# Split buffers of g in two pools, one key scaling a step sooner, attention of block 0 in 27 half steps, and one block's output stores on another queue

## The chip, the cores and the metric

The kernel runs on one core of a Trainium2 chip. The metric is the device time of one execution in microseconds (us). The five engines that matter are TensorE (PE in the profile; its weight loads are PEld), VectorE (DVE), ScalarE (ACT), GpSimd (POOL) and SyncE (SP, which here only issues transfers). Each engine works through its own list of instructions in order, and an instruction that has to wait holds up everything behind it on that engine. ACT and SP both issue transfers (ACTq and SPq in the rows).

## The reference, cut to what matters

```python
# attention with decay: 4 sequences of 576 tokens, 8 heads of 64
scores = scale * np.matmul(q, k.transpose(0, 1, 3, 2))
Dmat = np.where(rel >= 0, gamma[:, None, None] ** rel[None, :, :], 0.0)
ret = scores * Dmat[None, :, :, :]
attn_out = np.matmul(ret, v)
x = attn_out.transpose(0, 2, 1, 3).reshape(B * S, H * D)      # 2304 x 512
# layer one, 512 -> 2048 -> 512
h = x @ w_in;  g = h * (1.0 / (1.0 + np.exp(-h)));  x = g @ w_out
# layer two, the same sizes with its own weights
h = x @ w_in;  g = np.maximum(h, 0.0) ** 2;         out = g @ w_out
```

## The kernel before, in words

The 2304 tokens are cut into 18 *units* of 128 tokens. Attention is computed unit by unit with a running state S (`scores_step`: products of keys and queries into P, mask, new state; `values_step`: products with the values into Q, which become a unit's columns of x).

Products that must keep fp32 accuracy are done in three float32r passes: each operand is split into a high part (`xh`, `gh`, `wi`; a cast on ACT) and a low part (`xl`, `gl`; a subtraction on DVE or POOL), and TensorE adds high*high, high*low and low*high. Where the program has a helper for this it is `split` (L690 to L692): a cast on ACT at once, and a subtraction that is put on the list `later`/`low` and emitted with the next work.

**Layer one, first part.** Three *blocks* of tokens, `BLOCKS = [512, 384, 384]` (units 0 to 3, 4 to 6, 7 to 9). For each block and each of 16 slices f of the hidden width, `gemm1` makes `ph` (12 matmuls, L83), ACT and DVE gate and split it, and two slices later `gemm2` adds it to `acc` (12 matmuls, L83). Each slice has two *half steps*: `gemm1` stands ahead of the first, `gemm2` in the second. During block 0 the weights are converted from 64-bit numbers, one tile each half step: stage a (two ACT operations, L115 and L116), b (three DVE operations, L121 to L123), c (ACT cast, L135), d (DVE subtraction, L139). The attention of the next block's units runs beside the current block: `run_att` does as many attention steps as the fraction of half steps that has passed. Block 0 carries the six steps of units 4 to 6, whose x is the input of block 1.

`prep_k(u)` scales the keys of unit u: one POOL operation (L351) for one half of the heads and four ACT operations (L354) for the other. The second group of products in `scores` (L369) needs them; the first group (L364) doesn't. For unit 4 it stands in the loop over slices.

In the last slice of a block `gemm2` copies the four `acc` tiles to y (L665, DVE and ACT in turn) and ACT issues their stores (L666).

**Layer one, second part** (from about 302 us): the remaining 1024 tokens with seven block products in place of eight (L761), after sums and splits of x (`xsa`).

**Layer two** works in the same seven-product form. Its first phase (L901) makes g, which goes out to DRAM from the tiles `g` of pool "gq" (L940, `gD<-g`, on SP). Its second phase (L990) loads g back (`gr<-gD`, L952), sums and splits it (`sum_g`, `split_g`) and multiplies it with the split sums of the weights (`w2s`). There are 9 groups P of token rows with 7 products i each. Which split is emitted beside which product is decided by the small planner at the end: every entry has a step at which it is due and a cost, and each product adds 3.6 to the room. The tiles that `split_g` writes come from a pool "hl" of six buffers that is opened when x's pool "xp" and the pools of the first phase are closed; so these buffers lie where x and the g tiles lay, and the first instruction that writes one waits until the old content is no longer read.

Of the kernel before, what the change touches and what calls it, by code (L numbers as in the profile page):

```python
# [8 lines left out]
F32R = mybir.dt.float32r  # L9
# [15 lines left out]
KD, KF = DM // 128, DFF // 128  # L25
BLOCKS = [512, 384, 384]
# [17 lines left out]
def kernel(  # L44
# [16 lines left out]
    nc = tc.nc  # L61
# [18 lines left out]
    def mm3(o, pairs, first=True, last=True):  # L80
        n = len(pairs)
        for i, (a, b) in enumerate(pairs):
            mm(o, a, b, start=first and i == 0, stop=last and i == n - 1)  # L83
# [61 lines left out]
    def flush():  # L145
        now = later[:]
        later.clear()
        for emit in now:
            emit()
# [6 lines left out]
    def keep_w(n):  # L156
        layer, f, part = w_at(n)
        if part == 0:
            t = first.pop(n) if n in first else conv[n][0]
            nc.sync.dma_start(out=w1f[f // 2, :, f % 2], in_=t.bitcast(F32))  # L160
# [10 lines left out]
    def conv_to(layer, n):  # L171

        for i in range(conv_n[layer], min(n, 2 * KF + 2)):
            conv_n[layer] += 1
            for lag, stage in ((2, conv_c), (0, conv_a), (1, conv_b), (2, conv_d)):
                if 0 <= i - lag < 2 * KF:
                    stage(layer * 2 * KF + i - lag)
                    if stage is conv_b and n_loaded[0] < i - lag + layer * 2 * KF + RAW + 1:
                        load_next()
                    if stage is conv_b:  # L180
                        keep_w(i - lag)
# [53 lines left out]
    def pre_step():  # L235

        step = pre_n[0]
        pre_n[0] += 1
        for n, at in enumerate(pre_at):
            k = step - at  # L240
            if k == 0:
                pre_load(n)
            elif k == 2:
                conv_a(("p", n, 0))
            elif k == 3:
                conv_b(("p", n, 0))
                conv_a(("p", n, 1))
            elif k == 4:
                conv_b(("p", n, 1))
            elif k in (5, 6):  # L250
                pre_sums(n, k - 5)
            elif k == 7:
                pre_store(n)
# [71 lines left out]
    def load(u, queue=nc.sync):  # L325
        if u < NU:
            new_raw(u)
            for g in range(NG):
                queue.dma_start(out=raw[u][g], in_=att[NG * u + g])
# [15 lines left out]
    def prep_k(u):  # L345

        for g in range(NG):
            kn = raw[u][g][:, 256:512].rearrange("p (h d) -> p h d", h=4)
            w = (Tkn_u if u < n_start else Tkn)[:, 4 * g : 4 * g + 4]
            if g == 0 and u < u_end[1]:  # L350
                nc.gpsimd.tensor_mul(kn, kn, w.unsqueeze(2).to_broadcast([128, 4, D]))  # L351
            else:
                for h in range(4):
                    nc.scalar.activation(kn[:, h], kn[:, h], ACTF.Copy, scale=w[:, h : h + 1])  # L354
# [261 lines left out]
    x2 = dp.tile([128, KD, NT], F32, name="x2")  # L616
    tok0 = [sum(BLOCKS[:j]) for j in range(len(BLOCKS))]
    ph_t = {}

    def gemm1(layer, j, f, c0=0, c1=None):  # L620

        n = BLOCKS[j]
        c1 = c1 or n
        if c0 == 0:
            ph_t[layer, j, f] = ps_g.tile([128, 512], F32, tag="g", name="ph")[:, 0:n]
        ph = ph_t[layer, j, f][:, c0:c1]
        wh, wl = wt[0, f][:, 0], wt[0, f][:, 1]
        xh, xl = x_t[j]
        for k in range(KD):
            w0 = slice(k * 128, k * 128 + 128)  # L630
            mm3(
                ph,
                [(wh[:, w0], xh[:, k, c0:c1]), (wh[:, w0], xl[:, k, c0:c1]), (wl[:, w0], xh[:, k, c0:c1])],
                first=k == 0 and c0 == 0,
                last=k == KD - 1 and c1 == n,
            )
        if c1 == n:
            later.append(lambda: gate(layer, j, f, ph_t.pop((layer, j, f))))
# [11 lines left out]
    def gemm2(layer, j, f):  # L650
        n = BLOCKS[j]
        gh, gl = g_t.pop((layer, j, f))
        wh, wl = wt[1, f][:, 0], wt[1, f][:, 1]
        if f == 0:
            acc[layer, j] = [ps_o.tile([128, 512], F32, tag="o", name="acc") for _ in range(KD)]
        for t in range(KD):
            o = acc[layer, j][t][:, 0:n]
            w0 = slice(t * 128, t * 128 + 128)
            pairs = [(wh[:, w0], gh), (wh[:, w0], gl), (wl[:, w0], gh)]
            mm3(o, pairs, first=f == 0, last=f == KF - 1)  # L660
            if f == KF - 1:
                if t % 2 == 0:
                    ys = rp.tile([128, 2, 512], F32, tag="wr", name="y")
                y = ys[:, t % 2, 0:n]
                (nc.scalar.copy if t % 2 else nc.vector.tensor_copy)(y, o)  # L665
                nc.scalar.dma_start(out=x2[:, t, tok0[j] : tok0[j] + n], in_=y)  # L666

# [6 lines left out]
    pools = {}  # L676
# [13 lines left out]
    def split(dst, src, engine=nc.vector):  # L690
        nc.scalar.copy(dst[0], src)  # L691
        low.append(lambda: engine.tensor_sub(dst[1], src, dst[0]))  # L692
# [43 lines left out]
    def ts_step(p, k):  # L736
        if k == 0:
            ts_load(p)
        elif k in (2, 3):
            ts_sum(p, k - 2)  # L740
        elif k == 5:
            ts_split(p)
# [199 lines left out]
    def wait(n, emit):  # L942
        later.append(emit if n == 0 else lambda: wait(n - 1, emit))

    g_raw = {}
    g_s = {}
    g_l = {}
# [21 lines left out]
    def split_g(P, i, pool, engine=nc.vector):  # L969
        src = g_s[P][i]  # L970
        if pool == "w":
            parts = [wp.tile([128, 2, 512], F32R, tag="w", name="gl") for _ in range(2)]
            for e, t in enumerate(parts):
                split((t[:, 0], t[:, 1]), src[:, 512 * e : 512 * e + 512], engine)
        else:
            t = pools[pool].tile([128, 2, 1024], F32R, tag="h", name="gl")
            split((t[:, 0], t[:, 1]), src)
            parts = [t[:, :, 0:512], t[:, :, 512:1024]]
        g_l[P, i] = parts
# [76 lines left out]
    nb = len(BLOCKS)  # L1056
# [30 lines left out]
    def run_att(upto):  # L1087
        while pos[0] < min(upto, len(att_steps)):
            u, step = att_steps[pos[0]]
            step(u)  # L1090
            pos[0] += 1

    def att_end(j):
        return 2 * (u_end[j] - n_start)
# [55 lines left out]
    for i in range(len(seq) + LAG):  # L1150
        if i < len(seq):
            layer, j, f = seq[i]
            if i == 0:
                for c in ((0, AHEAD), (AHEAD, BLOCKS[0])):
                    for ff in range(2):
                        gemm1(layer, j, ff, *c)
            elif i > 1:
                gemm1(layer, j, f)
            if i == 0:
                for n in range(W1_FIRST):  # L1160
                    keep_w(n)
            if i == 1:
                load(n_start + 1)
            if i == 2:
                prep_k(n_start)
        for half in range(2):
            step = 2 * (i - (nb - 1) * KF) + half
            if step >= 0:
                flush()
            if i < len(seq):  # L1170
                if j == 0:
                    conv_to(0, 2 * f + half + 1 + W1_AHEAD)
                if j == 1 or step == 0:
                    pre_step()
                if j == 1 and half == 0:
                    nc.sync.dma_start(out=woD[f], in_=wt[1, f].bitcast(F32))
                if j == nb - 1:
                    for p in range(5):
                        ts_step(p, step - 4 * p - 3)
            if step >= 0:  # L1180
                strassen_x(step)
            if step < 0:
                flush()
            if half and i >= LAG:
                gemm2(*seq[i - LAG])
            if i < len(seq):
                a0, a1 = att_end(j), att_end(j + 1)
                run_att(a0 + (a1 - a0) * (2 * f + half + 1) // (2 * KF - 3 if j < nb - 1 else 22))
    flush()
    flush()  # L1190
    gp_ctx.close()
# [32 lines left out]
    for n in range(2 * KF):  # L1224
        h, f = divmod(n, KF)
# [19 lines left out]
    def new_pool(stack, name, bufs):  # L1245
        pools[name] = stack.enter_context(tc.tile_pool(name=name, bufs=bufs, reuse_waits="tile"))
# [28 lines left out]
    l1_ctx.close()  # L1275
    xp_ctx.close()
    lp_ctx.close()
    for name, bufs in (("hl", 6), ("rq", 6), ("tq", 1)):
        new_pool(ctx, name, bufs)


# [16 lines left out]
    for P in range(1, NPP):  # L1298
        n = 7 * P
# [6 lines left out]
    for P in range(1, NPP):  # L1306
        for q, at in ((2, -10), (3, -10), (0, -9), (1, -8)):
            pool, tag = ("w", "w") if q == 2 and P > 1 else ("rq", "r")
# [87 lines left out]
```

## Time and profile before

| | |
|---|---|
| time, median of 3 runs | 844.78 us (843.49 to 845.17) |
| the profiled execution, its own time | 838.52 us |
| span of the profile | 836.7 us |
| matmuls and weight loads | 6410 each |
| 128x512 fp32 products of one slice in block 0 | 12 for `ph`, 12 for `acc` |

The times of the rows below are us from the start of the span of this one execution. In a row of the timeline the first number is the start, the second the time from the start of the first to the end of the last instruction of the row, `x12` how many were merged, and the brackets at the end hold how long the engine sat idle before it and what released it. Instructions that only issue a transfer are not counted as busy time. PEclk is the clock that TensorE was granted, 1.00 for 2.4 GHz and 0.50 for 1.2 GHz.

### The profile page before, as it was taken

What the parts mean: (1) busy time and instruction counts of PE and PEld (TensorE: products, weight loads), DVE (VectorE), ACT (ScalarE), POOL (GpSimd) and SP (SyncE); (2) the same over time, 40 slices, a digit from 0 to 9 for tenths busy, and PEclk for the clock granted to TensorE, in tenths of its full rate; (3) what the DMA queues carried; (4) which work ended last, traced back from release to release, by engine and by line L of the source; (5) the groups of instructions that cost most, each with busy time, mean ns of one, the idle gap of its engine ahead of it and who ended that gap; (6) DMA issues with size and microseconds to landing.
All of it is one profiled execution on the core that took longest, in us unless ns stands there. A gap on an engine that the chain in (4) does not pass through costs nothing.

```text
span 836.7 us, 16174 instructions
## 1 busy us (share of the span) xinstructions
PE 812.1 (97%) x6410; PEld 751.6 (90%) x6410; DVE 548.0 (65%) x809; ACT 451.4 (54%) x862; POOL 186.0 (22%) x204
## 2 busy tenths in 40 slices
PE   6899999999999999999999999999999899999998
PEld 5788878999988988888888999999999789999998
DVE  5899994545434556666778577546477688777772
ACT  6777774454455455464555575646577434433430
POOL 3202012324544213213431222303254000000000
PEclk9989999999999999999999999999999999999999
DMA  9777775888534022698795465352676833444300
GB/s 353 255 229 240 253 225 201 310 308 298 190 128 153 1 78 87 222 313 309 225 344 184 154 225 165 122 171 92 202 275 213 310 139 126 140 134 136 122 27 26
DMA packets 71980, 160.70 MB, mean 192 GB/s; under 512 B 6112, under 2 KB 37344, under 8 KB 71904
## 3 DMA queue, kind: packets, MB, share of 16 engines
q1 hardware_dynamic: 66432, 149.44, 52.4%
q10 hardware_dynamic: 5472, 10.23, 3.3%
q8 instruction: 50, 0.82, 0.4%
q14 instruction: 26, 0.21, 0.1%
HBM read 104.07 MB, written 55.57 MB: 191 GB/s over the span
## 4 chain that ended last, share of the span: by engine, by line
PE 77%; DVE 3%; ACT 2%; issue 1%; DMA 1%; POOL 0%; ACTq 0%; DVEq 0%
PE acc L83 18%; PE pa L901 12%; PE pa L990 11%; PE pb L901 9%; PE pb L990 8%; PE ph L83 8%; PE pa L761 5%; PE pb L761 4%; PE Q L415 1%; DMA gD<-g 1%; PE P L364 1%; DVE xsa L692 1%; PE P L369 1%; ACT raw L354 1%; DVE gl L692 0%
## 5 line engine op out<-in xcount | busy, mean ns | idle before, releaser
L83 PE MATMUL ph<-xh,wi 128*128 128x384 f32 (+2 forms) x400 | 115.3, 351 | 1.3 <-ACT xh L457 1.3
L83 PE MATMUL acc<-gh,wo 128*128 128x384 f32 (+1 forms) x384 | 115.5, 362 | 0.0
L990 PE MATMUL pa<-w2s,gl 128*128 128x256 f32 x864 | 110.3, 285 | 4.0 <-ACT y L1005 3.0
L990 PEld LDWEIGHTS pa<-w2s,gl 128*128 128x128 f32 x864 | 107.1, 194 | 4.8 <-ACT y L1005 3.2
L901 PE MATMUL pa<-xa,w1s 128*128 128x384 f32 x576 | 105.9, 335 | 0.0
L901 PEld LDWEIGHTS pa<-xa,w1s 128*128 128x128 f32 x576 | 100.4, 188 | 0.1
L691 ACT CAST gl<-gr 128x1024 fp32r<-128x1024 f32 (+1 forms) x57 | 55.9, 1002 | 60.8 <-DVE gr L965 21.4
L83 PE MATMUL acc<-gsl,wo 128*128 128x512 f32 x384 | 87.7, 390 | 0.0
L83 PEld LDWEIGHTS acc<-gsl,wo 128*128 128x128 f32 x384 | 72.0, 188 | 15.5
L990 PE MATMUL pb<-w2s,gl 128*128 128x256 f32 x648 | 82.5, 283 | 1.6 <-ACT gl L691 0.8
L990 PEld LDWEIGHTS pb<-w2s,gl 128*128 128x128 f32 x648 | 79.7, 192 | 2.0 <-ACT gl L691 1.0
L901 PE MATMUL pb<-xa,w1s 128*128 128x384 f32 x432 | 80.9, 335 | 0.0
L83 PEld LDWEIGHTS ph<-xh,wi 128*128 128x128 f32 x400 | 73.2, 188 | 7.1 <-ACT xh L457 1.7
L83 PEld LDWEIGHTS acc<-gh,wo 128*128 128x128 f32 x384 | 71.8, 191 | 6.4
L901 PEld LDWEIGHTS pb<-xa,w1s 128*128 128x128 f32 x432 | 75.5, 188 | 0.1
L692 DVE TENSOR_TENSOR gl<-gr,gl 128x1024 fp32r<-128x1024 f32 (+1 forms) x55 | 64.7, 1181 | 13.5 <-ACT gl L691 13.5
L83 PE MATMUL ph<-xl,wi 128*128 128x384 f32 (+2 forms) x200 | 69.6, 348 | 0.3 <-DVE xl L461 0.3
L83 PE MATMUL acc<-gl,wo 128*128 128x384 f32 (+1 forms) x192 | 68.7, 358 | 0.0
L115 ACT ACTIVATE t<-wr 128x512 f32<-128x512 f32 x64 | 43.0, 672 | 26.6 <-DMA wr<-w 26.4
L648 DVE TENSOR_TENSOR gl<-sg,gh 128x384 fp32r<-128x384 f32 (+1 forms) x48 | 29.9, 623 | 40.5 <-ACT gh L647 40.5
L645 ACT ACTIVATE sg<-ph 128x384 f32<-128x384 f32 (+1 forms) x48 | 25.1, 524 | 53.1 <-PE ph L83 52.6
L122 DVE CUSTOM_DVE_ANT_0 t<-wr,t 128x1024 uint16<-128x1024 uint16 x64 | 47.6, 744 | 8.0 <-ACT sg L645 0.5
(140 smaller groups left out, 1334.5 us busy)
## 6 DMA issues: line engine op xcount, KB each, us to landing
wr<-w SPq DMA_DIRECT2D x64, 512.0 KB, 4.5
gD<-g SPq DMA_DIRECT2D x48, 384.0 KB, 2.8
gr<-gD SPq DMA_DIRECT2D x36, 512.0 KB, 4.7
raw<-att SPq DMA_DIRECT2D x32, 512.0 KB, 4.9
woD<-wo SPq DMA_DIRECT2D x16, 512.0 KB, 8.3
wo<-woD SPq DMA_DIRECT2D x16, 512.0 KB, 6.6
w2r<-w2c SPq DMA_DIRECT2D x14, 512.0 KB, 6.0
xq<-x SPq DMA_DIRECT2D x12, 384.0 KB, 5.7
```

Source lines behind the costliest of these rows:

```text
L83: mm(o, a, b, start=first and i == 0, stop=last and i == n - 1)
L115: nc.scalar.activation(t.bitcast(F32), hi.bitcast(F32), ACTF.Abs, scale=2.0**-112)
L122: nc.vector.tensor_tensor(t, t, lo, op=ALU.add)
L354: nc.scalar.activation(kn[:, h], kn[:, h], ACTF.Copy, scale=w[:, h : h + 1])
L364: mm(o, dims(u, a, e, b, 768), dims(u, a, e, b, 0), start=True, stop=True)
L645: nc.scalar.activation(s, ph, ACTF.Silu)
L648: later.append(lambda: nc.vector.tensor_sub(gl, s, gh))
L691: nc.scalar.copy(dst[0], src)
L692: low.append(lambda: engine.tensor_sub(dst[1], src, dst[0]))
L761: mm(o, lhs, rhs, start=m == 0 and i in (0, 1, 4), stop=m == 5, skip_group_check=True)
L901: mm(o, lhs, rhs, start=m == 0 and i in (0, 1, 4), stop=m == 5, skip_group_check=True)
L990: mm(o, lhs, rhs, start=first, stop=m == NP - 1 and q == 2, skip_group_check=True)
```

## The change

Four edits, here whole:

```diff
@@ gemm2: stores of the last of the three blocks
-                nc.scalar.dma_start(out=x2[:, t, tok0[j] : tok0[j] + n], in_=y)
+                queue = nc.sync if j == len(BLOCKS) - 1 else nc.scalar
+                queue.dma_start(out=x2[:, t, tok0[j] : tok0[j] + n], in_=y)
@@ split_g: the tile of a split
-            t = pools[pool].tile([128, 2, 1024], F32R, tag="h", name="gl")
+            t = pools["ha" if n_split[0] % 6 < 4 else "hb"].tile([128, 2, 1024], F32R, tag="h", name="gl")
+            n_split[0] += 1
@@ the loop over slices
             if i == 1:
                 load(n_start + 1)
-            if i == 2:
                 prep_k(n_start)
@@
-                run_att(a0 + (a1 - a0) * (2 * f + half + 1) // (2 * KF - 3 if j < nb - 1 else 22))
+                run_att(a0 + (a1 - a0) * (2 * f + half + 1) // (27, 29, 22)[j])
@@ pools of the second phase of layer two
-    for name, bufs in (("hl", 6), ("rq", 6), ("tq", 1)):
+    for name, bufs in (("ha", 4), ("hb", 2), ("rq", 6), ("tq", 1)):
```

Four buffers of 8 KB cover what x's pool took, so "ha" lies over x alone and "hb" over tiles g of the first phase. Both pools together have the six buffers of "hl", and a buffer is still taken again after six splits. `2 * KF - 3` is 29, so only block 0's number changes: its six attention steps come at half steps 5, 9, 14, 18, 23 and 27 where they came at 5, 10, 15, 20, 25 and 29.

On ACT, early in block 0, the scaling of unit 4's keys stood behind the conversion of two weight tiles (L135 is stage c, L115 and L116 are stage a); before:

```order
L647 CAST gh<-sg 128x512
L135 CAST wi<-t 128x512
L115 ACTIVATE t<-wr 128x512
L116 ACTIVATE wr<-wr 128x512
L135 CAST wo<-t 128x512
L115 ACTIVATE t<-wr 128x512
L116 ACTIVATE wr<-wr 128x512
L354 ACTIVATE raw<-raw,cs 128x64 x4
```

The same place of the changed kernel:

```order
L647 CAST gh<-sg 128x512
L354 ACTIVATE raw<-raw,cs 128x64 x4
L135 CAST wi<-t 128x512
L115 ACTIVATE t<-wr 128x512
L116 ACTIVATE wr<-wr 128x512
L135 CAST wo<-t 128x512
```

The four operations L354 passed six conversion operations, which are now behind them.

On DVE, at the end of block 0, the work on unit 6's attention output (Q, then xl, the low part of x that block 1 needs) stood behind the last weights (wo); before:

```order
L139 TENSOR_TENSOR wo<-t,wo 128x512
L648 TENSOR_TENSOR gl<-sg,gh 128x512
L121 TENSOR_SCALAR t<-t 128x512
L122 ISA t<-wr,t 128x1024
L123 SCALAR_TENSOR_TENSOR t<-wr,t 128x512
L139 TENSOR_TENSOR wo<-t,wo 128x512 x2
L648 TENSOR_TENSOR gl<-sg,gh 128x512
L454 TENSOR_TENSOR Q<-Q,xs 64x4x64 x2
L461 TENSOR_TENSOR xl<-Q,xh 128x4x128
```

The same place of the changed kernel, from the same L139 on:

```order
L139 TENSOR_TENSOR wo<-t,wo 128x512
L648 TENSOR_TENSOR gl<-sg,gh 128x512
L454 TENSOR_TENSOR Q<-Q,xs 64x4x64 x2
L121 TENSOR_SCALAR t<-t 128x512
L122 ISA t<-wr,t 128x1024
L123 SCALAR_TENSOR_TENSOR t<-wr,t 128x512
L139 TENSOR_TENSOR wo<-t,wo 128x512
L461 TENSOR_TENSOR xl<-Q,xh 128x4x128
L139 TENSOR_TENSOR wo<-t,wo 128x512
```

Q moved ahead of the last conversion and xl ahead of the last wo and a gl; all that stands ahead of the first row shown is the same set of operations in both kernels.

On ACT, at the start of layer two's second phase (gl<-gs is the second split that takes a buffer of the six, y the copy that frees TensorE's bank pa), with the semaphores that each waits for; before:

```order
L691 CAST w2s<-w2r 128x512 [waits DVE_49]
L691 CAST gl<-gs_6714 128x1024 [waits DMAHW7_49,DMAHW3_49,DMAHW2_49]
L691 CAST w2s<-w2r 128x512 [waits DMAHW6_49,DVE_49]
L691 CAST w2s<-w2r 128x512 [waits DVE_49]
L1005 COPY y<-pa 128x256 [waits PE_49]
```

The same place of the changed kernel, whose lines are numbered by up to three higher:

```order
L692 CAST w2s<-w2r 128x512 [waits DVE_49]
L692 CAST gl<-gs_6714 128x1024
L692 CAST w2s<-w2r 128x512 [waits DMAHW6_49,DVE_49]
L692 CAST w2s<-w2r 128x512 [waits PE_49]
L1008 COPY y<-pa 128x256 [waits PE_49]
```

The order is the same; the split no longer waits for three transfers (stores `gD<-g`), and the second w2s behind it waits for TensorE instead of DVE.

## Rows read from the trace of the kernel before

**Rows 1.** The page, busy time, share of the span and instructions by engine.
```profile
PE 812.1 (97%) x6410; PEld 751.6 (90%) x6410; DVE 548.0 (65%) x809; ACT 451.4 (54%) x862; POOL 186.0 (22%) x204
```

**Rows 2.** Waits of TensorE: line and what it waited for, us, times, longest.
```profile
PE pa L990 <- ACT y L1005: 3.0, 1, 3.0
PE P L369 <- ACT raw L354: 2.6, 1, 2.6
...
PE ph L83 <- ACT xh L457: 1.3, 1, 1.3
PE pa L761 <- ACT s L768: 1.3, 1, 1.3
```

**Rows 3.** Timeline of TensorE in block 0, units 4 and 5.
```profile
36.81 0.69 PE L364 MATMUL P<-raw 64*64 64x64 f32 x32
...
46.49 0.40 PE L83 MATMUL ph<-xh,wi 128*128 128x512 f32 x1
...
72.41 0.69 PE L364 MATMUL P<-raw 64*64 64x64 f32 x32
...
76.36 0.39 PE L83 MATMUL ph<-xh,wi 128*128 128x512 f32 x1
```

**Rows 4.** Busy time by stretch: us; PE PEld DVE ACT POOL; PEclk, DMA share, GB/s.
```profile
40.00:44.00 4.00, 3.68 (x15) 2.80 (x16) 3.69 (x8) 1.41 (x6) 0.00 (x0) 0.50 0.85 270
44.00:124.00 80.00, 80.00 (x620) 65.50 (x619) 74.47 (x126) 62.92 (x120) 9.84 (x11) 0.98 0.76 237
124.00:128.00 4.00, 2.41 (x12) 1.65 (x11) 2.82 (x6) 1.70 (x3) 0.00 (x0) 1.00 0.97 377
656.00:660.00 4.00, 2.04 (x9) 2.04 (x10) 3.37 (x5) 4.00 (x8) 0.00 (x0) 0.68 0.96 389
```

**Rows 5.** Timeline of ACT and POOL around the scaling of unit 4's keys.
```profile
34.87 0.62 ACT L647 CAST gh<-sg 128x512 fp32r<-128x512 f32 x1
...
39.68 1.06 ACT L354 ACTIVATE raw<-raw,cs 128x64 f32<-128x64 f32 x4
...
32.24 0.84 POOL L351 TENSOR_TENSOR raw<-raw,cs 128x256 f32<-128x256 f32 x1 [7.21 <-ACT cs L302]
```

**Rows 6.** Timeline of DVE, then of TensorE, at the end of block 0.
```profile
116.22 0.69 DVE L139 TENSOR_TENSOR wi<-t,wi 128x512 fp32r<-128x512 f32 x1
...
119.30 0.69 DVE L648 TENSOR_TENSOR gl<-sg,gh 128x512 fp32r<-128x512 f32 x1
119.90 0.42 DVE L121 TENSOR_SCALAR t<-t 128x512 int32<-128x512 int32 x1
...
121.78 0.68 DVE L139 TENSOR_TENSOR wo<-t,wo 128x512 fp32r<-128x512 f32 x1
...
124.65 0.90 DVE L454 TENSOR_TENSOR Q<-Q,xs 64x256 f32<-64x256 f32 x2
126.20 0.69 DVE L461 TENSOR_TENSOR xl<-Q,xh 128x512 fp32r<-128x512 f32 x1 [0.65 <-ACT xh L457]
...
119.31 0.39 PE L83 MATMUL ph<-xh,wi 128*128 128x512 f32 x1
...
126.95 0.45 PE L83 MATMUL ph<-xl,wi 128*128 128x384 f32 x1 [0.28 <-DVE xl L461]
```

**Rows 7.** Timeline of ACT and its queue behind the last block's products.
```profile
306.61 0.81 ACTq L666 DMA_DIRECT2D x<-y  x2
...
308.39 1.08 ACT L768 COPY s<-pa 128x512 f32<-128x512 f32 x2 [0.40 <-ACT y L665]
```

**Rows 8.** Timeline at layer two's second phase, and landing of the w2r loads there.
```profile
651.93 3.04 PE L990 MATMUL pb<-w2s,gl 128*128 128x256 f32 x24
...
655.55 1.04 ACT L691 CAST gl<-gs 128x1024 fp32r<-128x1024 f32 x1 [5.16 <-DMA gD<-g]
...
657.96 4.41 PE L990 MATMUL pa<-w2s,gl 128*128 128x256 f32 x24 [2.98 <-ACT y L1005]
...
DMA to landing us min/median/max: 4.9/8.1/11.0
```

More of the change, by code (lines that the diff above doesn't have):

```diff
@@ L943, in wait @@
         later.append(emit if n == 0 else lambda: wait(n - 1, emit))
+    n_split = [0]
     g_raw = {}
```

## Prediction

> **What bounds the kernel now.** I read the share of busy time first, then the list of what TensorE waited for, then each of those waits in the timeline, and last the busy time by stretch, because a share over the whole span is a mean over stages with different limits.
>
> TensorE is busy 97% of the span and DVE 65% [rows 1]. So what can be won lies in TensorE's waits and in stretches of low clock. Of its single long waits the four edits aim at four [rows 2]: 3.0 us at the start of layer two's second phase, 2.6 us for unit 4's keys, 1.3 us for unit 6's x ahead of block 1, and 1.3 us behind block 2. After the 2.6 us wait the granted clock was 0.50, the lower of its two levels, and around the 3.0 us wait its mean was 0.68; after the 1.3 us wait ahead of block 1 it stayed at 1.00 [rows 4]. A removed wait can therefore be worth more than its own length.
>
> In block 0 a second engine stands close to its limit. From 44 to 124 us DVE is busy 74.47 of 80 us, almost as TensorE is [rows 4], since it converts a weight tile every half step. That decides what the first two edits are worth.
>
> **Unit 4's keys.** From the first product of scores to the next ph takes 46.49 - 36.81 = 9.68 us for unit 4, and 76.36 - 72.41 = 3.95 us for unit 5, where nothing waits [rows 3]. The wait and the low clock behind it cost 5.73 us. The four operations take 1.06 us and started at 39.68; moved to just behind the cast that begins at 34.87 and takes 0.62, they end near 36.6 [rows 5], and the products that need them came at about 37.3. POOL's half was scaled at 32.24, after a wait for ACT's tables and not for a load [rows 5], so the unit's tiles were there. What now comes 1.06 us later is the conversion of two tiles on ACT; they are covered as long as DVE has work from earlier tiles, and if not, cost at most that 1.06 us. TensorE so leaves this place up to 5.73 us earlier.
>
> It can't keep that lead. At the end of block 0 the last ph starts at 119.31, and DVE finished its weights at 116.22 + 0.69 = 116.91 [rows 6]: 2.4 us of slack. The low part is needed by the third of the twelve matmuls, 0.4 us into them, so ph can start 2.8 us earlier and no more. The rest of the lead turns into short waits for weights in the second half of the block. Two bounds for the keys alone: nothing, if the input of block 1 sets the end of the block anyway, and 5.73 us, if DVE also moved ahead.
>
> **27 half steps.** Block 1 starts when xl of unit 6 is there: its matmul began at 126.95 after a wait for DVE [rows 6]. Up to gl at 119.30 the list of DVE holds the same operations in both kernels, and DVE has no idle time worth counting there, so I keep 119.30 and its successor's start at 119.90. Then come, in the new order: Q, 0.90 (the row at 124.65) and about 0.05 to the next; a conversion, 121.78 - 119.90 = 1.88; one wo, 0.60 to its successor; xl, 0.69. The sum is 119.90 + 0.95 + 1.88 + 0.60 + 0.69 = 124.0, where it was 126.20 + 0.69 = 126.9 [rows 6]. Block 1 starts 2.9 us earlier. TensorE arrives 2.8 us earlier than before, at about 122.1 instead of 124.9 (126.95 less the two waits of 1.3 and 0.3 us and a matmul), so it waits some 1.9 us there. The keys and the 27 belong together: without the keys TensorE would arrive at 124.9 and win 2.0; without the 27, xl comes at 126.9 as before and the keys win nothing. For both I take **2.9 us**; the bounds are 0, if the attention work that now stands ahead of three weight tiles delays DVE as much as it gains, and 5.73 + 1.6 = 7.3, if DVE's order sets nothing.
>
> What else moves with the 27: each values step issues the load of a later unit on SP and scales keys on ACT and POOL, all one or two half steps earlier; the loads stand between weight loads that TensorE needs four half steps later. They move, none is added, and I cost them at nothing; delayed by one 512 KB load the weights would come about 1.3 us later (4 us at 389 GB/s, as the row from 656 shows, is three such loads), which ACT would absorb, with 62.92 us of work in 80 [rows 4].
>
> **Stores on SP.** ACT spent 0.81 us on the issue of two stores between its copies and sat 0.40 us more, mostly on another, ahead of the copy s that TensorE waited for [rows 7]. These 1.21 us, and the 1.3 us wait of TensorE with them [rows 2], go away; the copies of y remain. On SP the four stores wait for the copies with the next weight loads for the second part behind them, and these wait for buffers that the same splits and copies free. I take **1.3 us**, all of the wait; the bounds are 0, if the copies alone keep ACT that long, and 1.3.
>
> **Two pools.** The second split sat 5.16 us on ACT for a store of g, and TensorE waited 2.98 us for the copy y two places behind it. The product then took 4.41 us where the one before took 3.04 [rows 8], at the low clock. Both together are 2.98 + 1.37 = 4.35 us. In the changed kernel the second to fourth split lie over x, whose last reader is the first phase. The split starts near 655.55 - 5.16 = 650.4. Next on ACT is a cast that needs the third of six loads w2r; with a median of 8.1 us from issue to landing [rows 8] it is there by about 651. Then y follows at about 653, ahead of the end of the product at 651.93 + 3.04 = 655.0. So nothing is late; the fifth split, the first in "hb", comes some 12 us later, when the stores have landed. I take **4.4 us**; the bounds are 0, if the w2r loads land as late as the slowest (11.0 us), and 4.4 plus the 2.5 us of smaller waits behind it, if those came only from ACT's delay. They seem to come from the order of DVE and ACT behind each product, so I leave them.
>
> **Sum.** 2.9 + 1.3 + 4.4 = 8.6 us. Against the profiled execution's own 838.52 that gives 829.9. The median of the timed runs is 6.3 us above that execution; the same difference taken off gives 844.78 - 8.6 = **836.2 us**.
>
> **Rivals.**
> *The clock falls at the new wait.* The 1.9 us ahead of block 1 lie between 1.3 us, after which the clock stayed up, and 2.6 us, after which it fell [rows 2, 4]. If it falls, the price is between 1.37 us (layer two) and 5.73 - 2.58 = 3.15 us (unit 4); with 2.3 the time is 838.5.
> *DVE takes the gain of block 0.* ACT's 1.06 us and the attention pieces ahead of the weights reach DVE's chain, which has no slack, and xl comes little earlier than before. Then 1.3 + 4.4 remain: 839.1.
> *The second phase waits for its weights instead.* The w2r loads set y's time, and only block 0 and the stores win: 844.78 - 4.2 = 840.6.
> *TensorE alone sets the pace.* Then every removed wait counts in full: 5.73 + 1.6 + 1.3 + 4.4 = 13.0, and 831.8. Against it stand DVE's 74.47 of 80 us [rows 4]. The Trainium skill, "Perfetto Trace Analysis", section "Identifying the Most-Contended Engine", would choose the engine by occupancy and, for TensorE, by the busy share of weight loads; over the whole span that is TensorE (90% against DVE's 65%), which would give this rival's time. The stretch of block 0 does not agree with it, and the page's section "Optimization Strategy" allows that the engine changes by regime.
> *Slower.* In the second half of block 0 TensorE, now ahead, stops for well under 1 us in front of each of the last six or so weight tiles. If the clock fell at each, at 3.15 us apiece, 18.9 us would go and the time would be 855. It decides at a wait of under 1 us; the clock of 1.00 after 1.3 us speaks against it [rows 4].
>
> **How the numbers follow.** Forecast 0.50, clock at the new wait 0.22, DVE takes the gain 0.12, second phase 0.07, TensorE alone 0.07, slower 0.02. The likeliest gives 836.2. The range from 832.8 to 841.0 holds the first four, with about 0.9 and some scatter of the runs, whose spread is 1.7 us; it leaves out most of the last two. A measurement of this kernel can tell about 0.2%, 1.7 us, from no change. Faster by more: 0.92, all cases but the last and a part of the weak ones. Within: 0.05. Slower: 0.03.
>
> **What will show it.** Right: no wait for raw L354 at the first scores, and clock 1.00 there; short waits of ph for wi from about 80 us on; ph of block 1 starting near 124 and waiting for xl; no wait of pa L761 for s; no idle ACT ahead of gl<-gs near 650, and seven products of equal length. Wrong: TensorE waiting for raw or weights before 60 us, xl not before 126, the clock at 0.50 behind 122, a wait of w2s for w2r in layer two.

## The result and the profile after

| | median, us | lowest to highest, runs |
|---|---|---|
| before | 843.13 | 840.23 to 845.17, 6 |
| changed kernel | 834.04 | 833.29 to 837.74, 6 |

The ratio is 0.990, with a 95% interval from 0.9874 to 0.9926: 8.4 us faster, between 6.2 and 10.6. A second set of runs of the changed kernel gave 834.81 us against 842.44, a ratio of 0.9913 (0.9889 to 0.9937). The forecast was 836.2 us, with a gain of 8.6.

The profiled execution of the changed kernel took 835.54 us. First the busy line of its page and, below it, TensorE's waits (line and what it waited for; us, times, longest); they answer to [rows 1, 2].

```profile
PE 809.6 (97%) x6410; PEld 749.4 (90%) x6410; DVE 548.7 (66%) x809; ACT 450.3 (54%) x862; POOL 187.4 (22%) x204
```

```profile
PE Q L415 <- DVE S L400: 4.7, 4, 1.6
...
PE P L364 <- issue: 2.2, 2, 1.5
...
PE pb L762 <- DVE u L773: 1.2, 1, 1.2
...
PE ph L83 <- ACT sg L645: 0.8, 1, 0.8
```

All four waits that the edits aimed at are gone. Some have come in their place: three inside block 0, where between 48 and 124 us there were none; one of 1.5 us ahead of the scores (P) of a unit; and one of 1.2 us behind block 2. The busy share of 97% is the same and tells nothing of this. (Lines of the changed kernel are numbered by up to three higher, so L1005 of [rows 2] is L1008 here.)

**Unit 4.** TensorE's timeline and then ACT's, as in [rows 3, 5], and the busy time by stretch, as in [rows 4]:

```profile
36.81 0.69 PE L364 MATMUL P<-raw 64*64 64x64 f32 x32
37.33 0.64 PE L369 MATMUL P<-raw 64*64 64x64 f32 x16
...
40.76 0.39 PE L83 MATMUL ph<-xh,wi 128*128 128x512 f32 x1
...
34.87 0.62 ACT L647 CAST gh<-sg 128x512 fp32r<-128x512 f32 x1
35.39 1.06 ACT L354 ACTIVATE raw<-raw,cs 128x64 f32<-128x64 f32 x4
```

```profile
40.00:44.00 4.00, 4.00 (x20) 3.30 (x19) 3.69 (x8) 0.72 (x2) 0.00 (x0) 1.00 0.90 279
44.00:124.00 80.00, 75.56 (x602) 61.08 (x601) 73.80 (x125) 61.99 (x119) 9.69 (x11) 1.00 0.79 249
```

The keys are scaled at 35.39 and the second group of scores follows the first at once. From the scores to the next ph it is 3.95 us where it was 9.68, at a clock of 1.00 where it was 0.50. But in the 80 us behind it TensorE is busy 75.56 us where it had no idle time, while DVE's busy time is nearly the same: the lead of 5.7 us is given back there.

**The end of block 0.** Timelines of DVE, ACT and TensorE, against [rows 6]:

```profile
116.36 0.69 DVE L139 TENSOR_TENSOR wi<-t,wi 128x512 fp32r<-128x512 f32 x1
...
118.23 0.69 DVE L123 SCALAR_TENSOR_TENSOR t<-wr,t 128x512 int32<-128x512 int32 x1
120.31 0.69 DVE L139 TENSOR_TENSOR wo<-t,wo 128x512 fp32r<-128x512 f32 x1 [1.38 <-ACT wo L135]
...
121.63 0.90 DVE L454 TENSOR_TENSOR Q<-Q,xs 64x256 f32<-64x256 f32 x2
...
125.17 0.69 DVE L461 TENSOR_TENSOR xl<-Q,xh 128x512 fp32r<-128x512 f32 x1
...
115.18 0.68 ACT L115 ACTIVATE t<-wr 128x512 f32<-128x512 f32 x1 [1.17 <-DMA wr<-w]
...
117.74 2.02 ACT L354 ACTIVATE raw<-raw,cs 128x64 f32<-128x64 f32 x8
119.67 0.60 ACT L135 CAST wo<-t 128x512 fp32r<-128x512 f32 x1
...
118.61 0.39 PE L83 MATMUL ph<-xh,wi 128*128 128x512 f32 x1
...
125.96 0.69 PE L364 MATMUL P<-raw 64*64 64x64 f32 x32 [1.47 <-issue]
126.45 0.68 PE L369 MATMUL P<-raw 64*64 64x64 f32 x32
127.05 0.44 PE L83 MATMUL ph<-xh,wi 128*128 128x384 f32 x1
```

Two things stand here that the working ahead of the result did not have. DVE sits idle for 1.38 us ahead of a wo, because ACT's cast of it stands behind eight operations L354: with the values step of unit 6 the scaling of unit 7's keys has moved forward too. (From unit 7 on, `prep_k` puts both halves of the heads on ACT, so there are eight operations and not four.) And ahead of ph there are now scores, P. The account under "The change" is incomplete: at half step 32 the count is 32 * 6 // 27 = 7, so block 0 carries a seventh step, the scores of unit 7. They start at 125.96, just after xl has been made from the Q whose place they seem to need.

**Behind block 2**, where the stores now go out on SP. Here TensorE multiplies split sums of x (`xsa`) with weights (`wi`) and split sums of weights (`wt`) into its banks pa and pb. ACT copies a product out as s, and DVE combines it with another product into u, and the bank that u reads can then take a further product. A `wt` is made from a load `tsr`, sums of it (`tss`, on POOL), ACT's cast and DVE's subtraction. Timelines of SP, POOL, ACT, DVE and TensorE, against [rows 7]:

```profile
305.00 2.16 SPq L667 DMA_DIRECT2D x<-y  x4
307.33 8.87 SPq L715 DMA_DIRECT2D tsr<-w1f  x3
...
311.21 0.73 POOL L724 TENSOR_TENSOR tss<-tsr 128x256 f32<-128x256 f32 x1 [33.98 <-DMA tsr<-w1f]
...
312.79 0.62 ACT L692 CAST wt<-tss 128x512 fp32r<-128x512 f32 x1 [2.29 <-POOL tss L725]
...
313.45 2.40 DVE L693 TENSOR_TENSOR wt<-tss,wt 128x512 fp32r<-128x512 f32 x2 [5.41 <-ACT wt L692]
315.77 1.28 DVE L773 TENSOR_TENSOR u<-pb,s 128x512 f32<-128x512 f32 x2
...
301.31 2.96 PE L762 MATMUL pa<-xsa,wi 128*128 128x512 f32 x12
...
316.51 3.02 PE L762 MATMUL pb<-xsa,wt 128*128 128x512 f32 x12 [1.15 <-DVE u L773]
```

and the same load, sum and first product in the kernel before:

```profile
307.47 8.64 SPq L714 DMA_DIRECT2D tsr<-w1f  x3
...
315.68 1.28 DVE L772 TENSOR_TENSOR u<-pb,s 128x512 f32<-128x512 f32 x2
...
301.98 2.96 PE L761 MATMUL pa<-xsa,wi 128*128 128x512 f32 x12
```

ACT is free earlier and the copy s is no longer waited for. But read the chain from the bottom: TensorE waits for the sum u, u stands on DVE behind two subtractions wt, these wait for ACT's casts, these for POOL's sums, and these for a load that SP issues at 307.33 behind the four stores. A new wait of 1.15 us has taken the place of the old one of 1.29. The stores have themselves made this chain later: counted from the first product, the load leaves at 307.33 - 301.31 = 6.02 us where it left at 307.47 - 301.98 = 5.49, and u starts at 14.46 where it started at 13.70.

**Layer two's second phase**, ACT and then TensorE, against [rows 8]:

```profile
650.39 1.04 ACT L692 CAST gl<-gs 128x1024 fp32r<-128x1024 f32 x1
...
652.38 0.36 ACT L1008 COPY y<-pa 128x256 f32<-128x256 f32 x1
...
654.90 3.04 PE L993 MATMUL pa<-w2s,gl 128*128 128x256 f32 x24
...
670.31 4.40 PE L993 MATMUL pb<-w2s,gl 128*128 128x256 f32 x22 [0.76 <-DVE gl L693]
```

The split starts at 650.39 without idle time ahead of it (forecast 650.4), y follows at 652.38 (forecast about 653), and the product that had waited 2.98 us runs on. A later product took 4.40 us at the low clock in this execution, behind the small waits for gl that the forecast left alone.

### The profile page after: what moved, and what is told of

Its sections match the earlier page's. It is cut to its first block, busy times and chain, and to the rows that moved or that the text cites. A ratio compares the mean times of both kernels' runs of the same rounds, so it can differ in the third digit from the quotient of the medians.

```text
span 833.8 us, 16177 instructions
## 1 busy us (share of the span) xinstructions
PE 809.6 (97%) x6410; PEld 749.4 (90%) x6410; DVE 548.7 (66%) x809; ACT 450.3 (54%) x862; POOL 187.4 (22%) x204
## 4 chain that ended last, share of the span: by engine, by line
PE 75%; DMA 4%; DVE 3%; ACT 2%; issue 1%; POOL 0%; SPq 0%; ACTq 0%; POOLq 0%; DVEq 0%
PE acc L83 15%; PE pa L902 12%; PE pa L993 11%; PE pb L902 9%; PE ph L83 9%; PE pb L993 8%; PE pa L762 4%; PE pb L762 3%; PE Q L415 2%; DMA w2c<-wt 1%; DMA w2r<-w2c 1%; DMA wr<-w 1%; PE P L364 1%; PE P L369 1%; DVE xsa L693 1%
## 5 line engine op out<-in xcount | busy, mean ns | idle before, releaser
L83 PE MATMUL acc<-gh,wo 128*128 128x384 f32 (+1 forms) x384 | 113.7, 357 | 0.0
L115 ACT ACTIVATE t<-wr 128x512 f32<-128x512 f32 x64 | 42.9, 671 | 27.6 <-DMA wr<-w 24.1
```

Of the source, the lines that this page charges most:

```text
L115: nc.scalar.activation(t.bitcast(F32), hi.bitcast(F32), ACTF.Abs, scale=2.0**-112)
```

## The experiments

Every one was timed beside the kernel before, whose medians in the three sets were 842.12 us (28 runs), 842.05 (17) and 842.44 (11). Differences below are the ratio times 842. Since whole times of one kernel scatter by 2 us and more, the profiles are compared by stages as well, each counted from a mark inside the execution:

- A: from DVE's last `wi` (L139) of block 0 to the first of the seven-product form's products (changed kernel: 116.36 to 301.31)
- B: from there to the first product with `gsl`, the split of the next product's input (to 379.98)
- C: from the first product with `w2s` of layer two to the end of the span (643.40 to 833.75)

| kernel | profiled execution, us | A | B | C |
|---|---|---|---|---|
| before | 838.52 | 185.76 | 78.76 | 193.42 |
| keys | 840.93 | 185.78 | 78.77 | 194.92 |
| stores | 842.07 | 185.83 | 78.75 | 195.28 |
| h27 | 840.60 | 184.61 | 78.77 | 195.01 |
| keys27 | 839.68 | 184.63 | 78.77 | 194.49 |
| pools | 837.56 | 187.32 | 78.77 | 188.66 |
| changed | 835.54 | 184.95 | 78.67 | 190.35 |
| after2 | 835.19 | 184.54 | 78.86 | 188.56 |
| cap7 | 833.72 | 184.37 | 78.83 | 188.99 |
| late7 | 832.49 | 183.14 | 78.99 | 189.28 |
| ufirst | 838.02 | 184.49 | 77.20 | 190.06 |
| best | 832.41 | 183.15 | 77.22 | 188.59 |
| best_actstores | 831.76 | 183.09 | 78.77 | 188.55 |
| best_latekeys | 833.03 | 183.15 | 77.22 | 191.06 |

### One edit alone

`pools`, `keys`, `h27` and `stores` are the kernel before with one of the four edits of the diff above.

> Only the two pools of the second phase of layer two. Theory (the prediction's): the second split no longer waits 5.16 us on ACT for a store of g, TensorE loses neither its wait of 2.98 us nor the 1.37 us of low clock behind it: 4.4 us faster, 838.7 against a median of 843.1. Rival one: the split's weights (loads w2r) come late instead, and the time stays within 1 us. Rival two: smaller waits behind it came from ACT's delay too: up to 6.9 us faster.

Measured 836.61 us, ratio 0.9934 (0.9922 to 0.9946): 5.6 us faster, 4.5 to 6.6. Rival one is out. The waits for gl behind the place are still there, so rival two is not the reason for what is over 4.4. C shows one: 193.42 us in the execution that the forecast was read from, but 194.49 to 195.28 in the four others that keep the one pool. The wait for y and the time that the product behind it takes over 3.04 us come to 4.35 us in the profile of before and to 4.58 to 5.85 in those four (`keys` least, `keys27` most). And the clock can fall once more behind the small waits. In `keys`, busy time by stretch with TensorE alone (us; PE; PEclk, DMA share, GB/s):

```profile
660.00:690.00 30.00, 27.66 (x201) 0.90 0.46 163
```

and the same in `pools`:

```profile
660.00:690.00 30.00, 27.59 (x223) 1.00 0.56 212
```

The clock falls there in three of the five profiles with the long wait, as a second fall, and in three of the nine without that wait; among these nine C is 190.05 us or more where it falls and 189.28 or less where it doesn't. So few profiles don't show that the long wait makes this fall likelier. C is 188.55 to 191.06 us in the nine kernels with two pools, mean 189.3, and in the five with one pool the mean is 194.6. The difference of 5.3 us lies within the interval of the measured gain.

> Only unit 4's keys scaled a tile sooner. Theory: TensorE leaves the first scores 5.7 us earlier with the clock at 1.00, and gives all of it back in short waits for weights and in one wait for xl ahead of block 1, because DVE's order is unchanged and sets the end of block 0: 0 us, within 0.5. Rival one: TensorE alone sets the pace: 5.7 us faster. Rival two: the new waits let the granted clock fall: 2 us or more slower.

Measured 841.77 us, ratio 1.0004 (0.9989 to 1.0019): no change, from 0.9 us faster to 1.6 slower. TensorE is at ph 3.95 us after the scores, yet A is the same (185.78 us against 185.76) and xl comes 9.99 us after wi, as before (126.20 - 116.22 = 9.98). The theory holds, rival one is out, and the clock stayed at 1.00 through block 0.

> Only block 0's attention in 27 half steps. Theory: xl of unit 6 is there 2.9 us earlier, TensorE, which still waits for unit 4's keys, arrives only 0.9 us later than that and wins 2.0 us. Rival one: ACT's scaling of unit 7's keys, which now stands ahead of the last cast of block 0, and the seventh attention step, which now stands ahead of block 1, take back most of it: under 1 us. Rival two: 2.9 us or more, if TensorE's wait for the keys does not set its arrival.

Measured 840.43 us, ratio 0.9976 (0.9966 to 0.9986): 2.0 us, 1.2 to 2.9. The size is the theory's. The mechanism is only half of it: xl comes 8.79 us after wi, 1.2 earlier and not 2.9, and A falls by the same 1.2. The idle time of DVE that rival one names is in its trace:

```profile
121.73 0.69 DVE L139 TENSOR_TENSOR wo<-t,wo 128x512 fp32r<-128x512 f32 x1 [1.37 <-ACT wo L135]
```

> Only the output stores of the last block on SP. Theory: ACT is free 1.21 us earlier for the copy s and TensorE's wait of 1.3 us for it goes: 1.3 us faster. Rival (what the changed kernel's own profile hints at): the wait of a product for the copy s is replaced by one of about 1.2 us of the next product for a DVE sum, and nothing is won: within 0.3 us.

Measured 842.04 us, ratio 0.9995 (0.9980 to 1.0010). The rival holds: B is unchanged, and the wait of pb for u (1.22 us) stands in the place of that for s. The load of tsr leaves 6.02 us after the first product and u starts at 14.5, as in the changed kernel; in the profiles with the stores on ACT and the old order of u (before, `keys`, `h27`, `keys27`, `pools`) these are 5.48 to 5.49 and 13.7 to 13.95.

### Two edits, and the seventh step

> The keys and the 27 half steps together, without the stores and the pools. Theory one (the prediction's sum): they belong together and give 2.9 us, 839.2 against 842.1. Theory two (from the profiles of the single edits): the keys give nothing in any company, because DVE's conversions end the block; the 27 alone brought the low part of x 1.2 us earlier relative to DVE's chain, not 2.9, since the scaling of unit 7's keys stands ahead of a cast on ACT; so the two give what the 27 gave alone, 1.2 to 2.0 us, and the profile shows DVE idle for about 1.4 us ahead of a wo behind that cast.

Measured 838.78 us, ratio 0.9964 (0.9953 to 0.9976): 3.0 us, 2.0 to 4.0. By the sum theory one is right. By the trace theory two is: A is that of `h27`, and DVE is idle 1.21 us ahead of the wo. What the keys add to the 27 is 1.0 us by the medians of two sets, within their intervals; the profiles show 0.3 (below, `best_latekeys`). Whether the keys and the 27 are worth more together than apart stays open.

`cap7` is the changed kernel with

```diff
-                run_att(a0 + (a1 - a0) * (2 * f + half + 1) // (27, 29, 22)[j])
+                run_att(min(a0 + (a1 - a0) * (2 * f + half + 1) // (27, 29, 22)[j], a1))
```

> The changed kernel with the attention of block 0 ended after its six steps, so that the scores of unit 7 stand in block 1 again. Theory: TensorE waits for xl there anyway and does 1.1 us of scores only when a bank is free, behind that wait; moved into block 1 they cost the same 1.1 us, so nothing changes: within 0.4 us of the changed kernel (834.0 at its own runs). Rival: the scores fill a part of the wait now, and taking them out costs up to 1.1 us.

Measured 833.66 us, ratio 0.9904 (0.9884 to 0.9924), against 834.04 and 834.81 for the changed kernel. A is 184.37, against 184.95 and 184.54. The seventh step cost and gained next to nothing, 0.2 to 0.6 us in A: it fills no wait, and its products are only done at another time.

### What held the two weak terms back

`late7` is `cap7` with the scaling of unit 7's keys in block 1:

```diff
-        if u + 1 < NU:
+        if u + 1 < NU and u + 1 != u_end[1]:
             prep_k(u + 1)
...
                 prep_k(n_start)
+            if i == KF + 1:
+                prep_k(u_end[1])
```

> As the kernel before it in this call (no scores of unit 7 in block 0), and the scaling of unit 7's keys moved from the values step of unit 6 into the second slice of block 1, so that the cast of wo is not behind eight ACT operations of together 2.0 us. Theory: DVE's idle 1.38 us ahead of that wo goes, xl of unit 6 comes 1.4 us earlier, and the kernel is 1.4 us faster than the one without it, 832.6. Rival: the weights' loads, behind the loads of raw on SP, keep ACT and DVE just as late, and nothing is won; TensorE's own arrival at the end of the block is the bound, and under 0.5 us is won.

Measured 833.14 us, ratio 0.9901 (0.9878 to 0.9925). The times alone can't tell it from `cap7`; the trace can. Timelines of DVE, ACT and TensorE:

```profile
118.57 0.69 DVE L123 SCALAR_TENSOR_TENSOR t<-wr,t 128x512 int32<-128x512 int32 x1
119.18 0.69 DVE L139 TENSOR_TENSOR wo<-t,wo 128x512 fp32r<-128x512 f32 x1
...
124.03 0.69 DVE L461 TENSOR_TENSOR xl<-Q,xh 128x512 fp32r<-128x512 f32 x1
...
118.22 0.62 ACT L135 CAST wo<-t 128x512 fp32r<-128x512 f32 x1
...
124.41 0.33 PE L83 MATMUL ph<-xh,wi 128*128 128x384 f32 x1
124.78 0.45 PE L83 MATMUL ph<-xl,wi 128*128 128x384 f32 x1
```

The cast starts 118.22 - 116.70 = 1.52 us after the last wi, where it was 119.67 - 116.36 = 3.31 in the changed kernel. DVE's wo follows its t without idle time, and xl comes 124.03 - 116.70 = 7.33 us after wi (before: 9.98). That is 2.65 of the 2.9 us of the forecast. A falls to 183.14, by 1.23, and does so in all four kernels with this edit. ACT's wait for wr is still there (1.33 us here) and costs nothing: by the trace the theory holds and the rival of the weight loads falls.

`ufirst` is the changed kernel with the subtractions of `wt` put off by two products, so that they stand behind the sums u on DVE:

```diff
-            ts_step(p, n - 1 - 6 * (p - 5))
+            ks = n - 1 - 6 * (p - 5)
+            now = len(later)
+            ts_step(p, ks)
+            if ks == 5:
+                subs = later[now:]
+                del later[now:]
+                for emit in subs:
+                    wait(2, emit)
```

> The changed kernel with the two subtractions that make wt, behind the last block's products, emitted two products later on DVE, so that the sums u are ahead of them. Theory: with the stores on SP the wait of 1.15 us of TensorE for u comes from these subtractions, which wait for a load of tsr; it goes, and the kernel is 1.2 us faster, 832.9, as the stores should have made it. Rival: the next thing is late instead (loads of wr that wait for buffers which these subtractions free), and the time stays within 0.4 us.

Measured 833.28 us, ratio 0.9906 (0.9883 to 0.9929), with runs from 831.76 to 838.02. By the whole time it can't be told from the changed kernel (834.04 and 834.81); the trace tells it. DVE and TensorE:

```profile
314.33 0.69 DVE L773 TENSOR_TENSOR u<-pb,s 128x512 f32<-128x512 f32 x1 [3.24 <-PE pb L762]
315.71 0.69 DVE L773 TENSOR_TENSOR u<-pb,s 128x512 f32<-128x512 f32 x1 [0.69 <-PE pb L762]
316.62 2.40 DVE L693 TENSOR_TENSOR wt<-tss,wt 128x512 fp32r<-128x512 f32 x2 [0.21 <-ACT wt L692]
...
318.23 2.88 PE L762 MATMUL pb<-xsa,wt 128*128 128x512 f32 x12
```

No wait is left in this stretch, and B falls from 78.7 to 77.20. The chain from the load to wt is as late as before, but nothing waits for it now.

### Both, and what the old edits are worth then

`best` has the edits of `late7` and `ufirst`; `best_actstores` is `best` with the stores on ACT, `best_latekeys` is `best` with unit 4's keys at `i == 2`; `after2` is the changed kernel again.

> Both follow-ups together on the changed kernel: no scores of unit 7 in block 0 and the scaling of unit 7's keys in block 1; and the sums u ahead of the subtractions that make wt. Theory: the two places are apart and their gains add, 1.2 to 1.4 us and 1.2 to 1.5 us by the stages of the profiles: 2.6 us faster than the changed kernel of the same call, about 831.4. Rival: the later stages give one of them back (TensorE then waits for a split of gs or for weights of the second product), and it is within 1.3 us of the changed kernel.

Measured 830.39 us, ratio 0.9862 (0.9841 to 0.9883). It is the fastest of all, 4.4 us under the changed kernel of the same set, more than the 2.6 expected; A fell by 1.4 and 1.8 against its two profiles, B by 1.4 and 1.6. What is over these lies in the scatter of both medians.

> The kernel with both follow-ups, but the last block's stores on ACT again. Theory: with u out of the way the stores on SP are what takes TensorE's wait for s away, so this one is 1.3 us slower than the one with them, and its profile has a wait of pa for s of 1.3 us again and none of pb for u. Rival: the stores on SP are worth nothing in any company: within 0.3 us.

Measured 832.96 us, ratio 0.9892 (0.9873 to 0.9911): 2.6 us slower than `best` by the medians, with intervals that just overlap. B is 78.77 again, 1.55 more, and the old wait is back:

```profile
306.57 3.06 PE L761 MATMUL pa<-xsa,wi 128*128 128x512 f32 x12 [1.29 <-ACT s L768]
```

So by stage B the stores on SP are worth nothing alone and 1.5 us with u out of the way; and moving u without them is worth nothing either, since B is then that of the kernel before.

> The kernel with both follow-ups, but unit 4's keys scaled a tile later again. Theory: in the kernel with follow-ups TensorE no longer waits for xl ahead of block 1, so its own arrival counts there and the 5.7 us lost at unit 4 are no longer all covered by DVE: the slack of 2.4 to 2.8 us in front of the last ph and the short waits for weights cover most, and 0.5 to 1.5 us remain; slower by that. Rival one: the keys count for nothing in any company: within 0.3 us. Rival two: 3 us or more slower, since little slack is left.

Measured 831.37 us, ratio 0.9872 (0.9851 to 0.9893): 1.0 us slower by medians whose intervals overlap. The trace speaks for rival one: A is the same, and from the first scores to the last wi it takes 79.72 us against 79.46 in `best`. Over all profiles the mean of that is 79.86 us in the five kernels with the late keys (79.41 to 80.16) and 79.54 in the nine with the early ones (79.32 to 79.92). By these the keys are worth about 0.3 us, which the overlap of the two groups leaves in doubt.

> The changed kernel again, unaltered, for comparison on the same chip and for a second profile of it. Theory: 834.0; its second phase of layer two takes 189 to 191 us from the first product to the end, the scores of unit 7 stand ahead of block 1 with a wait of about 1.5 us, and the wait of pb for u of 1.2 us is there again. The wait of acc for a split of gs, 0.5 us, which only one profile showed, is scatter and need not come again.

Measured 834.81 us. C is 188.56, A 184.54, the waits ahead of the scores (1.53 us) and of pb for u (1.3) are there, and that of acc for gsl is not.

## Why the prediction was right, and where not

**The time.** The 2.2 us between 836.2 and 834.04 are a matter of the level: the 844.78 us that the gain was taken from was a median of three runs, and the next sets gave 842.1 to 842.4. From 842.1 the same sum gives 833.5. That the gain of 8.6 us came so close to the measured 8.4 is in part luck: two terms were off in opposite directions, the stores by 0.9 us too much and the pools by 1.2 us too little, and a third had the right size by a wrong working. Measured apart, the parts add up to 3.0 + 0.4 + 5.6 = 9.0 us, within the interval of the whole (6.2 to 10.6).

**Unit 4's keys: right.** Where they were moved to, when they ran (35.39 to 36.45, forecast about 36.6), the clock behind them, and that alone they win nothing, all came as said; DVE's list and not TensorE sets the end of block 0. One detail is off: the waits in the block were forecast for wi. They stand ahead of P, Q and ph, and what ended them was DVE or ACT where the trace names it (0.75, 1.25 and 0.84 us at 64.74, 78.34 and 91.92).

**27 half steps: right sum, wrong working.** The step that failed is "xl comes 2.9 us earlier". It counted DVE's list alone. In the trace of `h27` and of the changed kernel xl came 1.2 us earlier, since ACT's cast of a wo stood behind L354 x8, 2.02 us, which the same edit had moved ahead of it. The prediction named these scalings and costed them at nothing, with ACT's busy share as the cover. A busy share of 0.8 covers no operation that stands directly ahead of one that is waited for; `late7` showed the price, 1.2 us. Nor did TensorE reach the end of block 0 2.8 us earlier: its last ph there came at 118.61 instead of 119.31, 0.7 us earlier, and the sign "ph of block 1 starting near 124" did not come; it started at 127.05, with 1.1 us of scores now ahead of it. Against that the measured 3.0 us for keys and 27 is more than the 1.2 us of A and the 0.3 us ahead of it, so its agreement with 2.9 does not bear out the working. Part of the rest can be the clock: of the four profiles with the old order, one (`pools`) has it fall behind the wait ahead of block 1, and none of the ten with the new order. Its timeline of TensorE and the stretch:

```profile
128.43 0.45 PE L83 MATMUL ph<-xh,wi 128*128 128x384 f32 x1 [1.85 <-ACT xh L457]
```

```profile
128.00:132.00 4.00, 3.29 (x10) 3.03 (x11) 1.39 (x2) 1.49 (x3) 0.00 (x0) 0.64 0.44 179
```

Its A is 1.5 us longer. How often that happens in the timed runs is not shown, so about 1 us of the 3.0 stays open, within its interval.

**Stores on SP: the term that was not there.** Here 1.3 us was forecast, with a lower bound of 0 for another reason (the copies keeping ACT). Measured is 0.4 us with an interval from 1.7 faster to 0.8 slower, and no change in B. The removed wait had covered a second chain, load, POOL, ACT, DVE, that ends in u. In the kernel before, u started 13.70 us after the first product, and the product that needs it follows 0.74 us behind; without waits TensorE would now come at 316.51 - 1.15 - 301.31 = 14.05. By this estimate about 0.4 us of the new wait would have stood there anyway, and the rest of the 1.15 came from the stores, behind which the load leaves later. The prediction named these loads behind the stores and gave the delay no cost, and it did not ask what stands in DVE's list at that place. `ufirst` and `best_actstores` show that the 1.5 us are there once that chain is out of the way.

**Two pools: mechanism right, size too small.** 4.4 us was forecast, 5.6 measured. The wait and the product behind it were read rightly, but from the execution that paid least for them of the five with one pool (4.35 us, the others 4.58 to 5.85), and it had no second fall of the clock, which three of the others had. The small waits stayed, as said.

**The rivals.** The clock stayed at 1.00 at the end of block 0 in every profile of the changed order, and the new waits of 0.75 to 1.25 us inside block 0 left it at 1.00 as well, so "slower" did not come either. "DVE takes the gain" was right that a delay on ACT reaches DVE's chain and takes over half of the 2.9 us from xl, but it named unit 4's keys as the delay, and it was unit 7's. The second phase's weights were in time. "TensorE alone sets the pace", 831.8 us, is the figure nearest below, but for the wrong reason: the keys alone would then have won 5.7 us and won nothing. The rule of the Trainium skill ("Perfetto Trace Analysis", "Identifying the Most-Contended Engine") that stood beside it picks TensorE when it is applied to the whole span, and the runs do not agree with that for block 0: there a 1.2 us change of ACT's and DVE's order moved the end, and a 5.7 us one of TensorE's did not. Applied to the 80 us of block 0 in [rows 4] alone, the same measures pick DVE, busy 74.47 us against 65.50 of weight loads, and with that the runs agree.

## What to carry to other kernels

When a wait goes, write down every chain that ends at the same instruction or just behind it, and when each ends: the second latest sets the gain. When a step is moved, follow all that it issues into the list of every engine, and look for what stands right behind it there; a low busy share hides nothing in a chain of cast and subtraction. Read stages from a mark inside the execution over several profiles, because one profile can miss a cost, such as a fall of the clock, that others pay.

## What the runs showed of the hardware

One DVE operation of 128x768 took 0.94 us in 12 profiles and 2.65 us in two, at the same place (here `after2`); the sum u behind it, and a product, came 1.5 us late each time.

```profile
580.14 2.66 DVE L857 TENSOR_TENSOR xq<-xq 128x768 f32<-128x768 f32 x1
```

In `best` DVE stood idle for 2.41 us with nothing in the profile to release it, and 8 us later TensorE waited for the split of gs:

```profile
442.61 3.69 PE L83 MATMUL acc<-gsl,wo 128*128 128x512 f32 x15 [1.07 <-DVE gsl L693]
...
434.70 0.43 DVE L121 TENSOR_SCALAR t<-t 128x512 int32<-128x512 int32 x1 [2.41 <-issue]
```

What causes either is not shown, nor that the first leads to the wait behind it. Both lie between B and C, from the first product with gsl to the first with w2s. That stretch took 262.6 us in all six profiles of before, the four single edits and `keys27`. In the eight of the changed kernel and its variants it took 262.6 to 264.6, and over 263 in five of them, the changed kernel's own two among these (263.42 and 264.34). No forecast had this, and whether the edits bring it about stays open.

The start scatters as well: the first scores of unit 4 came at 36.81 us in the profile of the changed kernel and at 40.56 in that of `ufirst`, with the same products of TensorE ahead of them. These 3.75 us, and the long DVE operation, are why `ufirst`, whose stage B is 1.5 us shorter, has a profile of 838.02 us.
